# Four additions a weight pair move from VectorE to GpSimd, and the weight preparation around them shifts by one to two products

## The chip, the cores and the metric

The kernel runs on one core of a Trainium2 chip. Its time is device microseconds (us) of one execution, as the median over several runs. The engines are called by the letters of the profile: PE is TensorE (matrix products; PEld its weight loads), DVE is VectorE, ACT is ScalarE, POOL is GpSimd and SP is SyncE, which issues the transfers (DMAs).

## The reference

Retention attention over 8 sequences of 8 heads, followed by two feed-forward layers over its 4608 tokens, all in float32:

```
x = attention(q, k, v)                      # [4608, 512]
h = x @ w_in                                # [4608, 2048]
x2 = (h * cos(h)) @ w_out                   # [4608, 512]
z = max(max(x2 @ w1, x2 @ w2), x2 @ w3)     # [4608, 768]
out = z @ w_out2                            # [4608, 512]
```

## The kernel before, in words

**Tiles.** Tokens go in 9 blocks of 512. Every large product works on 2x2 quarters of its operands with seven products in place of eight (the names A11, A12, A22, S1 to S4 are quarters and their sums and differences). Each operand is split into a high and a low float32r part, and three matmuls (high by high, low by high, high by low) make one term.

**Stages**, in us of the profiled span: lead-in to about 95; attention and the first half of h to 346; the second half of h to 596; **x2** from 596 to 1001; the three branches (w1, w2, w3) to about 1405; the last product to the end. The change acts in x2, and a little in the branches.

**x2** (`phase_out`, kind "wo") goes through 36 groups: 9 blocks by 4 groups (k = 0 to 3) of the 2048 features. A group is seven products of 12 matmuls, in the order A11, A12, S4, S2, A22, S3, S1. The names of a group's tiles end in its k: `k_g_2` holds the quarters of group 2 as loaded. `build_out` prepares a group while the group before it is multiplied:

- two loads of `k_g` (SP, L364); two differences `ta_g` on POOL (L350); the high part `x_g` of A11 (ACT L741) and its low part (DVE L745);
- high parts `h_g` (ACT L749) and low parts `l_g` (DVE L754), for A12 and S4 straight from `k_g`, for S2 and A22 from `tb_g`, for S3 and S1 from `ta_g`;
- `tb_g`, two differences on DVE (L350), the first of which reads the first half of `ta_g`.

`finish_out` combines finished products on DVE (L794) and ACT (L801).

**Background conversions.** While the large products run, `background` turns weight pairs of the later stages into the seven operands of such a product. There are 24 conversions. Twelve belong to earlier stages and end before the step that changes (`if (kind, i) in plain: return`). Of the other twelve, nine run in x2, one a block (tiles `raw_b`, `fa_b`, `p_b`), and three in the branches (`raw_o`, `fa_o`, `p_o`). One conversion:

- load the first half of the raw weights (L165); widen on ACT (L171, L172), join on DVE (L176, L177), total on POOL (L183); then the same with the second half, whose load waits until the first total has read the tile;
- `add_up`: four additions and subtractions of quarters, 128x256 each (`sums`, L190 to L193);
- four pieces k = 0 to 3: high part on ACT (L200, L204, L207), low part on POOL (L216; L212 on DVE for k = 1), and a store to DRAM (L261).

**What sets the order.** `at(n, fn)` puts a step into a table and `tick()` closes a product: steps `at(n)` are issued n products from now, and within one product in the order in which they were entered. Each engine then works strictly in the order of issue, so a step that waits holds up all that stands behind it on its engine.

Of the kernel before, what the change touches and what calls it, by code (L numbers as in the profile page):

```python
# [101 lines left out]
def retention_ffn(ctx: ExitStack, tc: tile.TileContext, att, w_in, w_out, w123, w_out2, cst, out):  # L102
    nc = tc.nc
# [8 lines left out]
    def w14(name, dt=F32R):  # L112
        shape = [128, 7, 2, HB] if dt == F32R else [128, 7 * NB]
        return wpool.tile(shape, dt, tag="w", name=name)

    def x4(name, shape, dt=F32):
        return xpool.tile([128, *shape], dt, tag="x", name=name)
# [4 lines left out]
    def f32(t):  # L122
        return t.bitcast(F32)
# [13 lines left out]
    def at(n, fn):  # L137
        agenda.setdefault(slot[0] + n, []).append(fn)
# [25 lines left out]
    def load_raw(raw, kind, i, n):  # L164
        nc.sync.dma_start(out=raw, in_=source(kind, PAIRS[kind][i][n]).bitcast(U32))  # L165

    def widen(raw, t):

        r = raw.rearrange("p (n t) -> p n t", t=2)
        low, high = r[:, :, 0], r[:, :, 1]  # L170
        nc.scalar.activation(t.bitcast(F32), high.bitcast(F32), AF.Copy, scale=2.0**-111)  # L171
        nc.scalar.activation(low, low, AF.Copy, scale=2.0**-29)  # L172

    def join(raw, t):
        high = raw.rearrange("p (n t) -> p n t", t=2)[:, :, 1]
        nc.vector.tensor_scalar(out=t, in0=t, scalar1=3, scalar2=None, op0=ALU.logical_shift_left)  # L176
        nc.vector.scalar_tensor_tensor(  # L177
            out=high, in0=high, scalar=0x80000000, in1=t, op0=ALU.bitwise_and, op1=ALU.bitwise_or
        )

    def total(raw, dst, eng):
        r = raw.rearrange("p (n t) -> p n t", t=2)
        eng.tensor_tensor(out=dst.bitcast(U32), in0=r[:, :, 0], in1=r[:, :, 1], op=ALU.add)  # L183

    def quarters(kind, fa):
        return [fa[:, q] for q in PLACES[kind]]

    def sums(kind, fa, s, eng):
        a11, a12, a21, a22 = quarters(kind, fa)
        eng.tensor_tensor(out=s[:, 0], in0=a21, in1=a22, op=ALU.add)  # L190
        eng.tensor_tensor(out=s[:, 1], in0=s[:, 0], in1=a11, op=ALU.subtract)
        eng.tensor_tensor(out=s[:, 2], in0=a11, in1=a21, op=ALU.subtract)
        eng.tensor_tensor(out=s[:, 3], in0=a12, in1=s[:, 1], op=ALU.subtract)  # L193

    def piece_high(kind, fa, s, k, dst):

        if k == 0:
            step = PLACES[kind][1]
            src = fa[:, 0 : 2 * step : step] if step > 1 else fa[:, 0:2]
            nc.scalar.copy(dst[:, :, 0], src)  # L200
            return src
        if k == 1:
            src = quarters(kind, fa)[3]
            nc.scalar.activation(dst[:, 0, 0], src, AF.Copy, scale=-1.0)  # L204
            return src
        src = s[:, 2 * k - 4 : 2 * k - 2]
        nc.scalar.copy(dst[:, :, 0], src)  # L207
        return src

    def piece_low(k, src, dst, eng):  # L210
        if k == 1:
            nc.vector.scalar_tensor_tensor(  # L212
                out=dst[:, 0, 1], in0=src, scalar=-1.0, in1=f32(dst[:, 0, 0]), op0=ALU.mult, op1=ALU.subtract
            )
        else:
            eng.tensor_tensor(out=dst[:, :, 1], in0=src, in1=f32(dst[:, :, 0]), op=ALU.subtract)  # L216
# [5 lines left out]
    def background(kind, i, arena):  # L222

        st = {}

        def begin():
            if arena:
                w = w14(f"ar_{kind}{i}", F32)
                st["raw"] = w[:, : 2 * NB].bitcast(U32)
                st["fa"] = w[:, 2 * NB : 4 * NB].rearrange("p (q n) -> p q n", q=4)  # L230
                st["t"] = w[:, 6 * NB :].bitcast(U32)
            else:
                st["raw"] = x4(f"raw_{kind}{i}", [2 * NB], U32)
                st["fa"] = x4(f"fa_{kind}{i}", [4, HB])
                st["t"] = spare
            load_raw(st["raw"], kind, i, 0)

        def convert(n):
            return [
                lambda: widen(st["raw"], st["t"]),  # L240
                lambda: join(st["raw"], st["t"]),
                lambda: total(
                    st["raw"], st["fa"][:, 2 * n : 2 * n + 2].rearrange("p q n -> p (q n)"), nc.gpsimd
                ),
            ]

        def add_up():
            st["s"] = f32(st["raw"]).rearrange("p (q n) -> p q n", q=4)
            sums(kind, st["fa"], st["s"], nc.vector)

        def high(k):
            lo, hi = PIECE[k]
            st["p", k] = x4(f"p_{kind}{i}_{k}", [hi - lo, 2, HB], F32R)
            st["src", k] = piece_high(kind, st["fa"], st["s"], k, st["p", k])

        def low(k):
            piece_low(k, st["src", k], st["p", k], nc.gpsimd)

        def keep(k):
            lo, hi = PIECE[k]  # L260
            nc.sync.dma_start(out=stash[kind, i][:, lo:hi], in_=f32(st["p", k]))  # L261

        c0, c1 = convert(0), convert(1)
        at(0, begin)
        for n, fn in enumerate(c0):
            at(3 + n, fn)
        at(6, lambda: load_raw(st["raw"], kind, i, 1))
        for n, fn in enumerate(c1):
            at(9 + n, fn)
        if (kind, i) in plain:  # L270
            at(13, lambda: nc.sync.dma_start(out=plain[kind, i], in_=st["fa"]))
            return
        at(14, add_up)
        for k in range(4):
            at(15 + k, lambda k=k: high(k))
            at(16 + k, lambda k=k: low(k))
            at(18 + k, lambda k=k: keep(k))

    def split_pair(kind, i, fa, s):
        w = w14(f"w_{kind}{i}")  # L280
# [44 lines left out]
    def raw_operand(o, product):  # L325
        return {
            P_A11: lambda: o["k1"][:, 0],
            P_A12: lambda: o["k2"][:, 0],
            P_S4: lambda: o["k2"][:, 1],
            P_S1: lambda: o["ta"][:, 0],  # L330
            P_S3: lambda: o["ta"][:, 1],
            P_S2: lambda: o["tb"][:, 0],
            P_A22: lambda: o["tb"][:, 1],
        }[product]()
# [17 lines left out]
    def high(o, product):  # L352
        x = o[product] = x4(f"x_{o['name']}_{product}", [2, o["n"]], F32R)
        nc.scalar.copy(x[:, 0], raw_operand(o, product))

    def low(o, product, eng):
        x = o[product]
        eng.tensor_tensor(out=x[:, 1], in0=raw_operand(o, product), in1=f32(x[:, 0]), op=ALU.subtract)  # L358
# [335 lines left out]
    for j in range(1, NBLK):  # L694
        k = 4 * (j - 1)
        build_in(block_of(j), start_of(k + 1) + 7, start_of(k + 3) + 7, xsd[j], nc.gpsimd)
    back = [(k, i) for k, n in (("wi", 4), ("wo", 0), ("b", 0), ("o", 0)) for i in range(n, len(PAIRS[k]))]
    per = 14
    for j in range(NBLK - 2):
        at(per * j, lambda: background(*back.pop(0), True))  # L700
# [16 lines left out]
    for j in range(NBLK - 1):  # L717
        at(endA + per * j + 3, lambda j=j: load_operands(j + 1))
        if j < 5:
            at(endA + per * j + 1, lambda: background(*back.pop(0), True))  # L720
# [140 lines left out]
            ),  # L861
        )
    for i in range(len(back) - 3):
        at(28 * i + 5, lambda: background(*back.pop(0), False))
    for k in range(4):
        for p in range(2):
            at(28 * (NBLK - 1) + 7 * k + 8 + p, lambda k=k, p=p: take("b", 2 * k + p))
# [113 lines left out]
```

## Time and profile before

| | |
|---|---|
| median of 3 runs | 1564.41 us (1562.49 to 1566.82) |
| the profiled execution | 1566.85 us, span 1565.0 us |
| PE busy in the span | 1468.8 us (94%) |
| DVE busy | 1233.1 us (79%) |
| ACT busy | 728.8 us (47%) |
| POOL busy | 493.4 us (32%) |

Shares of the whole span mix stages with different limits; the stage x2, from 596 to 1001, is the one to read. In the rows below a timeline's row gives start and duration, both in us, then engine, line, operation and tiles, and in brackets the idle time of the engine ahead of it and what ended that. Rows of waits give the idle time in total, how often, and the longest. The names of operands carry no group number there; where a row belongs to a certain group, the text says so.

### The profile page before, as it was taken

How to read it: one execution, taken by the hardware profiler on the slowest of the kernel's cores; microseconds unless marked ns; L12 is line 12 of the kernel's file. 1: busy time of each engine (PE TensorE's matmuls, PEld its weight loads, DVE VectorE, ACT ScalarE, POOL GpSimd, SP SyncE). 2: the span in 40 equal slices, each digit the busy share in tenths (PEclk: the TensorE clock that was granted, in tenths of full speed). 3: DMA queues.
4: the chain of work that ended last, by engine and by line, in shares of the span. 5: the costliest groups of instructions: out<-in, count | busy, mean ns of one | idle time of the engine just before them, and what ended most of it. 6: DMA issues, size and time to landing. Idle time of an engine off the chain costs nothing. (4 is left out here: it accounts for less than half of the span.)

```text
span 1565.0 us, 30902 instructions
## 1 busy us (share of the span) xinstructions
PE 1468.8 (94%) x12506; PEld 1424.4 (91%) x12506; DVE 1233.1 (79%) x1611; ACT 728.8 (47%) x1214; POOL 493.4 (32%) x364
## 2 busy tenths in 40 slices
PE   7799999997998996899999999999999999998998
PEld 5698989996988996899999999899999999998998
DVE  6988989898878869899999999746554554538997
ACT  4465655565666665344443444434433333323332
POOL 3544444434333334455444445201110000003221
PEclk9999999997999997999999999999999999999999
DMA  7588888875998873545556656944332211153543
GB/s 287 202 307 316 313 295 301 304 256 212 330 339 303 326 276 132 183 165 177 191 188 209 206 168 253 390 176 142 129 100 83 68 46 50 68 193 137 176 164 133
DMA packets 83086, 324.47 MB, mean 207 GB/s; under 512 B 9216, under 2 KB 9216, under 8 KB 76928
## 3 DMA queue, kind: packets, MB, share of 16 engines
q1 hardware_dynamic: 82944, 322.51, 58.0%
q8 instruction: 98, 1.61, 0.4%
q14 instruction: 44, 0.36, 0.1%
HBM read 190.35 MB, written 132.12 MB: 206 GB/s over the span
## 5 line engine op out<-in xcount | busy, mean ns | idle before, releaser
L781 PE MATMUL wo<-h_g,w_wo 128*128 128x256 f32 x1728 | 317.9, 285 | 0.0
L781 PEld LDWEIGHTS wo<-h_g,w_wo 128*128 128x128 f32 x1728 | 273.0, 194 | 0.0
L781 PE MATMUL wo<-l_g,w_wo 128*128 128x256 f32 x864 | 250.3, 290 | 20.7 <-DVE l_g L754 20.1
L379 PE MATMUL d_b<-x_z,w_b 128*128 128x256 f32 x1944 | 250.1, 284 | 7.0 <-DVE s_b L403 4.9
L379 PEld LDWEIGHTS d_b<-x_z,w_b 128*128 128x128 f32 x1944 | 241.2, 193 | 7.9 <-DVE s_b L403 5.1
L781 PEld LDWEIGHTS wo<-l_g,w_wo 128*128 128x128 f32 x864 | 167.6, 194 | 27.3 <-DVE l_g L754 27.0
L446 POOL TENSOR_SCALAR t_a<-t_a 128x1024 f32<-128x1024 f32 x72 | 91.9, 1281 | 179.9 <-DVE t_a L445 138.2
L379 PE MATMUL d_a<-x_x,w_wi 128*128 128x256 f32 x864 | 126.1, 298 | 9.3 <-DVE x_x L358 7.4
L379 PE MATMUL b_b<-x_z,w_b 128*128 128x256 f32 x972 | 131.9, 284 | 2.0 <-DVE x_z L358 2.0
L379 PE MATMUL d_a<-x_y,w_wi 128*128 128x256 f32 x864 | 116.0, 292 | 18.5 <-DVE s_a L403 7.9
L379 PEld LDWEIGHTS d_a<-x_y,w_wi 128*128 128x128 f32 x864 | 110.5, 199 | 21.6 <-DVE s_a L403 8.1
L379 PEld LDWEIGHTS d_a<-x_x,w_wi 128*128 128x128 f32 x864 | 113.0, 199 | 14.2 <-DVE x_x L358 8.5
L379 PEld LDWEIGHTS b_b<-x_z,w_b 128*128 128x128 f32 x972 | 123.5, 192 | 2.2 <-DVE x_z L358 2.2
L350 POOL TENSOR_TENSOR ta_m<-k_m 128x512 f32<-128x512 f32 (+1 forms) x18 | 18.9, 1048 | 334.0 <-DMA k_m<-mq 273.6
L749 ACT CAST h_g<-tb_g 128x1024 fp32r<-128x1024 f32 x36 | 37.8, 1049 | 179.6 <-DVE tb_g L350 174.1
L781 PE MATMUL o<-h_m,w_o 128*128 128x256 f32 x648 | 117.4, 283 | 0.0
L453 DVE TENSOR_TENSOR s_a<-s_a,t_a 128x1024 f32<-128x1024 f32 x72 | 98.7, 1385 | 15.4 <-ACT t_a L450 15.1
L403 DVE TENSOR_TENSOR s_b<-s_b,b_b 128x512 f32<-128x512 f32 (+1 forms) x45 | 28.5, 634 | 93.7 <-PE b_b L379 92.1
L781 PEld LDWEIGHTS o<-h_m,w_o 128*128 128x128 f32 x648 | 101.1, 192 | 0.0
L445 DVE SCALAR_TENSOR_TENSOR t_a<-s_a,t_a 128x1024 f32<-128x1024 f32 x72 | 97.6, 1375 | 0.4 <-ACT t_a L441 0.4
L450 ACT ACTIVATE t_a<-t_a 128x1024 f32<-128x1024 f32 x72 | 75.7, 1060 | 46.5 <-POOL t_a L446 46.5
L350 POOL TENSOR_TENSOR ta_g<-k_g 128x512 f32<-128x512 f32 x36 | 51.5, 1431 | 128.5 <-DMA k_g<-gq 128.5
(168 smaller groups left out, 3200.0 us busy)
## 6 DMA issues: line engine op xcount, KB each, us to landing
u<-att SPq DMA_DIRECT2D x36, 1024.0 KB, 8.1
gq<-s_a SPq DMA_DIRECT2D x72, 512.0 KB, 6.7
k_g<-gq SPq DMA_DIRECT2D x72, 512.0 KB, 6.6
xs<-x_x SPq DMA_DIRECT2D x63, 512.0 KB, 8.0
x_y<-xs SPq DMA_DIRECT2D x63, 512.0 KB, 7.7
w_b<-st_b SPq DMA_DIRECT2D x8, 1792.0 KB, 14.0
st_b<-p_b SPq DMA_DIRECT2D x27, 512.0 KB, 2.9
raw_b<-w SPq DMA_DIRECT2D x18, 512.0 KB, 5.6
```

What stands on the lines that cost most here:

```text
L350: eng.tensor_tensor(out=d, in0=a, in1=b, op=ALU.subtract)
L379: nc.tensor.matmul(h[:, p * HB : (p + 1) * HB], a, b, start=first and p == 0 and i == 0, stop=i == len(terms) - 1, skip_group_check=True,)
L403: nc.vector.tensor_tensor(out=dst, in0=dst, in1=b[:, :n], op=ALU.add)
L445: nc.vector.scalar_tensor_tensor(out=r, in0=s, scalar=INV2PI, in1=st["t"], op0=ALU.mult, op1=ALU.subtract)
L446: nc.gpsimd.tensor_scalar(out=r, in0=r, scalar1=R_MOST, scalar2=R_LEAST, op0=ALU.min, op1=ALU.max)
L450: nc.scalar.activation(r, r, AF.Sin, scale=TURN, bias=HALF_PI)
L453: nc.vector.tensor_tensor(out=s, in0=s, in1=f32(st["t"]), op=ALU.mult)
L749: nc.scalar.copy(h, o[pairs[k][2]])
L781: nc.tensor.matmul(b[:, mt * HB : (mt + 1) * HB], a, v, start=first and mt == 0 and p == 0 and i == 0, stop=last and p == len(ws) - 1 and ...
```

## The change

The four sums of `add_up` are issued on POOL in place of DVE (12 conversions, 48 instructions). The four pieces come later: the high part of piece k at 16, 17, 19, 20 products from the conversion's start in place of 15 to 18, and low part and store likewise. The nine conversions of x2 start two products earlier within their block; those in the branches start where they did.

```
         def add_up():
             st["s"] = f32(st["raw"]).rearrange("p (q n) -> p q n", q=4)
-            sums(kind, st["fa"], st["s"], nc.vector)
+            sums(kind, st["fa"], st["s"], nc.gpsimd)
...
         at(14, add_up)
         for k in range(4):
-            at(15 + k, lambda k=k: high(k))
-            at(16 + k, lambda k=k: low(k))
-            at(18 + k, lambda k=k: keep(k))
+            at(16 + k + k // 2, lambda k=k: high(k))
+            at(17 + k + k // 2, lambda k=k: low(k))
+            at(19 + k + k // 2, lambda k=k: keep(k))
...
     for i in range(len(back) - 3):
-        at(28 * i + 5, lambda: background(*back.pop(0), False))
+        at(28 * i + 3, lambda: background(*back.pop(0), False))
```

POOL, from the differences of group 1 to the first low part, in one block of x2 before (a row is line, operation, tiles, shape):

```order
266 L350 TENSOR_TENSOR ta_g_1_9166<-k_g_1_9102 128x512
267 L350 TENSOR_TENSOR ta_g_1_9166<-k_g_1_9104,k_g_1_9102 128x512
268 L350 TENSOR_TENSOR ta_g_2_9285<-k_g_2_9224 128x512
269 L350 TENSOR_TENSOR ta_g_2_9285<-k_g_2_9226,k_g_2_9224 128x512
270 L183 TENSOR_TENSOR fa_b_9244<-raw_b_9243 128x512
271 L350 TENSOR_TENSOR ta_g_3_9404<-k_g_3_9344 128x512
272 L350 TENSOR_TENSOR ta_g_3_9404<-k_g_3_9346,k_g_3_9344 128x512
273 L183 TENSOR_TENSOR fa_b_9244<-raw_b_9243 128x512
274 L216 TENSOR_TENSOR p_b_0_9492<-fa_b_9244,p_b_0_9492 128x2x256
```

The same stretch of POOL after the change:

```order
288 L183 TENSOR_TENSOR fa_b_9208<-raw_b_9207 128x512
289 L350 TENSOR_TENSOR ta_g_2_9290<-k_g_2_9227 128x512
290 L350 TENSOR_TENSOR ta_g_2_9290<-k_g_2_9229,k_g_2_9227 128x512
291 L183 TENSOR_TENSOR fa_b_9208<-raw_b_9207 128x512
292 L350 TENSOR_TENSOR ta_g_3_9405<-k_g_3_9344 128x512
293 L350 TENSOR_TENSOR ta_g_3_9405<-k_g_3_9346,k_g_3_9344 128x512
294 L190 TENSOR_TENSOR raw_b_9207<-fa_b_9208 128x256
295 L191 TENSOR_TENSOR raw_b_9207<-raw_b_9207,fa_b_9208 128x256
296 L192 TENSOR_TENSOR raw_b_9207<-fa_b_9208 128x256
297 L193 TENSOR_TENSOR raw_b_9207<-fa_b_9208,raw_b_9207 128x256
298 L216 TENSOR_TENSOR p_b_0_9478<-fa_b_9208,p_b_0_9478 128x2x256
```

Each of the two totals (L183) stood behind the differences `ta_g` of a group and now stands ahead of them; the four sums now follow the differences of group 3.

DVE before, from the last low part of group 2 to the low parts of group 3:

```order
888 L754 TENSOR_TENSOR l_g_2_9374<-ta_g_2_9285,h_g_2_9341 128x1024
889 L176 TENSOR_SCALAR spare<-spare 128x512
890 L177 SCALAR_TENSOR_TENSOR raw_b_9243<-raw_b_9243,spare 128x512
891 L745 TENSOR_TENSOR x_g_3_9407<-k_g_3_9344,x_g_3_9407 128x512
892 L350 TENSOR_TENSOR tb_g_3_9437<-k_g_3_9346,ta_g_3_9404 128x512
893 L754 TENSOR_TENSOR l_g_3_9439<-k_g_3_9346,h_g_3_9423 128x1024
894 L350 TENSOR_TENSOR tb_g_3_9437<-tb_g_3_9437,k_g_3_9346 128x512
895 L190 TENSOR_TENSOR raw_b_9243<-fa_b_9244 128x256
896 L191 TENSOR_TENSOR raw_b_9243<-raw_b_9243,fa_b_9244 128x256
897 L192 TENSOR_TENSOR raw_b_9243<-fa_b_9244 128x256
898 L193 TENSOR_TENSOR raw_b_9243<-fa_b_9244,raw_b_9243 128x256
899 L754 TENSOR_TENSOR l_g_3_9478<-tb_g_3_9437,h_g_3_9454 128x1024
```

The same stretch of DVE after:

```order
868 L176 TENSOR_SCALAR spare<-spare 128x512
869 L177 SCALAR_TENSOR_TENSOR raw_b_9207<-raw_b_9207,spare 128x512
870 L754 TENSOR_TENSOR l_g_2_9378<-ta_g_2_9290,h_g_2_9342 128x1024
871 L745 TENSOR_TENSOR x_g_3_9408<-k_g_3_9344,x_g_3_9408 128x512
872 L350 TENSOR_TENSOR tb_g_3_9441<-k_g_3_9346,ta_g_3_9405 128x512
873 L754 TENSOR_TENSOR l_g_3_9443<-k_g_3_9346,h_g_3_9423 128x1024
874 L350 TENSOR_TENSOR tb_g_3_9441<-tb_g_3_9441,k_g_3_9346 128x512
875 L754 TENSOR_TENSOR l_g_3_9480<-tb_g_3_9441,h_g_3_9458 128x1024
```

The second join (L176, L177) now comes ahead of the last low part of group 2, and the four sums are gone. The first join has likewise moved ahead of the `x_g` of group 2 (it stood behind it), and on ACT the first widening (L171, L172) stands ahead of the high parts `x_g` and `h_g` of group 2, directly behind the two `h_g` of group 1. On SP the first raw load goes out ahead of the `k_g_2` loads in place of behind them.

## Rows read from the trace of the kernel before

**Rows 1.** The page: busy time by engine, and a costly group of instructions.

```profile
PE 1468.8 (94%) x12506; PEld 1424.4 (91%) x12506; DVE 1233.1 (79%) x1611; ACT 728.8 (47%) x1214; POOL 493.4 (32%) x364
...
L781 PE MATMUL wo<-l_g,w_wo 128*128 128x256 f32 x864 | 250.3, 290 | 20.7 <-DVE l_g L754 20.1
```

**Rows 2.** Busy time by stretch: PE, PEld, DVE, ACT, POOL; clock, DMA share, GB/s.

```profile
872.79:915.99 43.20, 42.07 (x336) 41.86 (x336) 39.93 (x41) 19.02 (x25) 20.70 (x13) 0.96 0.56 190
...
898.33:915.99 17.66, 16.53 (x138) 16.32 (x137) 17.59 (x18) 6.87 (x10) 12.09 (x8) 1.00 0.35 126
```

**Rows 3.** Waits of DVE from 872.79 to 915.99.

```profile
DVE l_g L754 <- ACT h_g L749: 2.3, 2, 1.2
```

**Rows 4.** Timeline of PE: A12 and S4 of group 3, A12 of the next block.

```profile
904.38 0.40 PE L781 MATMUL wo<-h_g,w_wo 128*128 128x256 f32 x2
...
905.82 0.40 PE L781 MATMUL wo<-h_g,w_wo 128*128 128x256 f32 x2
...
915.99 0.39 PE L781 MATMUL wo<-l_g,w_wo 128*128 128x256 f32 x1 [1.14 <-DVE l_g L754]
```

**Rows 5.** Timeline of DVE, from 884 to 909.

```profile
884.02 1.93 DVE L754 TENSOR_TENSOR l_g<-tb_g,h_g 128x1024 fp32r<-128x1024 f32 x1 [1.17 <-ACT h_g L749]
885.87 2.32 DVE L754 TENSOR_TENSOR l_g<-ta_g,h_g 128x1024 fp32r<-128x1024 f32 x1
...
890.38 2.07 DVE L754 TENSOR_TENSOR l_g<-k_g,h_g 128x1024 fp32r<-128x1024 f32 x1
...
896.50 0.42 DVE L176 TENSOR_SCALAR spare<-spare 128x512 uint32<-128x512 uint32 x1
897.00 0.69 DVE L177 SCALAR_TENSOR_TENSOR raw_b<-raw_b,spare 128x512 uint32<-128x512 uint32 x1
...
901.19 2.06 DVE L754 TENSOR_TENSOR l_g<-k_g,h_g 128x1024 fp32r<-128x1024 f32 x1
903.17 0.68 DVE L350 TENSOR_TENSOR tb_g<-tb_g,k_g 128x512 f32<-128x512 f32 x1
903.77 0.41 DVE L190 TENSOR_TENSOR raw_b<-fa_b 128x256 f32<-128x256 f32 x1
...
905.23 1.22 DVE L754 TENSOR_TENSOR l_g<-tb_g,h_g 128x1024 fp32r<-128x1024 f32 x1
...
907.50 0.69 DVE L794 SCALAR_TENSOR_TENSOR o_wo<-wo,u_wo 128x512 f32<-128x512 f32 x1
```

**Rows 6.** Timeline of POOL, from 883 to 909.

```profile
883.57 1.30 POOL L350 TENSOR_TENSOR ta_g<-k_g 128x512 f32<-128x512 f32 x1 [3.61 <-DMA k_g<-gq]
...
889.99 1.36 POOL L183 TENSOR_TENSOR fa_b<-raw_b 128x512 uint32<-128x512 uint32 x1 [2.89 <-DVE raw_b L177]
...
898.98 1.74 POOL L350 TENSOR_TENSOR ta_g<-k_g,k_g 128x512 f32<-128x512 f32 x1
900.68 1.49 POOL L183 TENSOR_TENSOR fa_b<-raw_b 128x512 uint32<-128x512 uint32 x1
906.60 2.15 POOL L216 TENSOR_TENSOR p_b<-fa_b,p_b 128x512 fp32r<-128x512 f32 x1 [4.44 <-ACT p_b L200]
```

**Rows 7.** Timeline of ACT, from 883 to 905.

```profile
883.89 1.05 ACT L749 CAST h_g<-ta_g 128x1024 fp32r<-128x1024 f32 x1
...
887.03 0.68 ACT L172 ACTIVATE raw_b<-raw_b 128x512 uint32<-128x512 uint32 x1
...
903.94 1.05 ACT L749 CAST h_g<-tb_g 128x1024 fp32r<-128x1024 f32 x1 [4.02 <-DVE tb_g L350]
```

**Rows 8.** POOL groups by shape: busy us, mean ns; idle before.

```profile
L350 POOL TENSOR_TENSOR ta_m<-k_m,k_m 128x256 f32<-128x256 f32 x9 | 7.7, 851 | 1.2 <-DMA k_m<-mq 1.1
L350 POOL TENSOR_TENSOR ta_m<-k_m 128x256 f32<-128x256 f32 x9 | 7.1, 790 | 53.5 <-DMA k_m<-mq 33.6 <-PE o L781 13.0 <-DVE o_o L794 6.9
L183 POOL TENSOR_TENSOR fa_o<-raw_o 128x512 uint32<-128x512 uint32 x6 | 6.2, 1039 | 126.1 <-DVE raw_o L177 126.1
```

**Rows 9.** Waits from 1001 to 1380, the branches.

```profile
ACT x_z L354 <- DMA st_o<-p_o: 5.9, 3, 2.4
```

## Prediction

> **What bounds the kernel now.** The page comes first: TensorE is busy 94% of the span, so only what makes it wait, or ends waits, can count. Its costliest wait in x2 is for `l_g` from VectorE [rows 1]. The busy time by stretch says why: in one block, 872.79 to 915.99, VectorE works 39.93 us of 43.20 [rows 2]. A product that does not wait takes 1.44 us (A12 of group 3 begins at 904.38, the next at 905.82 [rows 4]), so the 28 products of a block need 40.3 us, and the block takes 43.2. VectorE's waits are the next view: 2.3 us of its idle time in that block are two waits for ScalarE's `h_g` [rows 3]; nothing it waits for comes from TensorE. And in the last 17.66 us of the block, the part that the change rebuilds, VectorE is busy 17.59 [rows 2]. The timeline of TensorE shows the end of this chain: the second product of the next block stands still until 915.99, when `l_g` is there [rows 4]. So VectorE sets the pace of x2, and whatever makes it later between 884 and 916 lengthens the block. Waits of the other engines need no more reading.
>
> One more reading decides the prices. VectorE and GpSimd stretch each other: `l_g` takes 1.22 alone (905.23) and 2.07, 2.06, 2.32 where GpSimd works at the same time [rows 5]; GpSimd's difference takes 1.30 at 883.57 and 1.74 at 898.98, its total 1.04 with VectorE elsewhere and 1.36 to 1.49 here [rows 6, 8]. The surplus is about the other engine's instruction. I read it as taking turns for instructions of VectorE with two tiles to read. L794, which reads one tile and a product's accumulator, keeps 0.69 at 907.50 within GpSimd's 2.15 us low part [rows 5, 6]. If the engines did not exclude each other, four sums of 0.65 to 0.85 (below) would take no turns from it, and of the 3.3 us a conversion that the walk below gives, 2.6 to 3.4 would be gone: the second rival. The Trainium skill, "SBUF — State Buffer", section "Who interferes with whom", has it that such an instruction of VectorE and one of GpSimd that reads shut each other out, the first to issue holding the other up for its whole length. By that rule the turns below stand, and the surplus in these rows agrees.
>
> **The change part by part.** Prices are net of the 0.08 us by which rows of one engine overlap (903.17 + 0.68 against 903.77): `l_g` 1.15, a 128x512 on VectorE 0.6, the join 0.5 + 0.6 [rows 5]; `ta_g` 1.3, the total 1.04 [rows 6, 8]; a widening of two 1.25, `h_g` 1.0 [rows 7]. The trace has no such sum on GpSimd. From below it is half of the 1.30 of a 128x512, 0.65; the nearest rows are differences of exactly 128x256, 0.79 and 0.85 on average, with collisions in them [rows 8]. I take 0.65 to 0.85.
>
> *The first total ahead of the differences of group 2.* Before, `ta_g_2` runs at 883.57, as soon as its quarters land, and the total waits for the join until 889.99 [rows 6]. Now GpSimd reaches `ta_g_2` only behind the total, and the total needs the join. The join is issued behind both `l_g` of group 1. These gain: without `ta_g_2` beside them, 884.02 + 2 × 1.15 = 886.3. Join to 887.4 (its widening follows ScalarE's `h_g` that ends at 884.94, done at 886.2 [rows 7], in time if the earlier raw load has landed, as it should). `x_g` to 888.0, total to 889.05, first difference to 890.35. Then `tb_g` 0.6, second difference 1.3 and `l_g` 1.15 take turns in some order: 893.4. Before, this `l_g` ended at 890.38 + 2.07 = 892.45. So **+0.95 us**; the cover is what group 1's `l_g` gained, without it it would be +2.9.
>
> *The second total ahead of the differences of group 3.* Second `tb_g` to 894.0, ScalarE's `h_g` to 895.1, `l_g` to 896.25, ScalarE's other `h_g` and the widening to 897.3, the join to 897.9 (before 897.69 [rows 5], but then with the last `l_g` of group 2 already done). From there `l_g` 1.15, `x_g` 0.6, total 1.04 and first difference 1.3 exclude each other: 902.0. `tb_g`, second difference and `l_g` as above: 905.05. GpSimd's first sum is ready by then and gets its turn ahead of `l_g` or not: 905.05 to 905.9, where `l_g` ended at 901.19 + 2.06 = 903.25. So **+1.8 to +2.65**, and TensorE, which began this A12 at 904.38 [rows 4], waits about a microsecond here.
>
> *The sums.* VectorE loses four instructions, 903.77 to 905.23, 1.46 us [rows 5]. But they lay in a gap: ScalarE's `h_g` from `tb_g` ran 903.94 to 904.99 [rows 7], and the next `l_g` began at 905.23. Taken out, they bring 0.2 us. On GpSimd they meet the second `tb_g` and the two `l_g` of group 3. From 905.7: `tb_g` 0.6, three further sums of 0.65 to 0.85, two `l_g` 2.3 in turns, 910.55 to 911.15; with the sums wholly inside ScalarE's wait, 909.65. Before, 907.50 + 0.08. So **+2.1 to +3.6**, I take +3.3, since GpSimd has the sums ready when `l_g` comes.
>
> *The pieces.* In x2 their first two come one product earlier, the others where they were. The low parts stay on GpSimd and still lie beside `l_g` and L212; drawn out from 1.30 alone they are already (2.15 [rows 6]). With less time between sums and pieces I add **0 to 0.6, take 0.3**. The stores are not waited for in x2.
>
> *The next block.* From 907.5 VectorE goes on without a pause to the `l_g` that TensorE awaits at 915.99 [rows 2, 4], so no slack eats the delay: about **+3.6 us a conversion, 32.4 for nine**.
>
> *The branches.* VectorE isn't the bound there, so four sums less bring nothing; the pieces come one to two products later. ScalarE waits three times, 5.9 us, for a stored piece to come back [rows 9]; most is covered by products already prepared. From below that stays so; from above that wait grows by half and TensorE sees all of it, 3 us. I take the middle, **+1.5**.
>
> Sum: 1566.85 + 32.4 + 1.5 = 1600.8 for the profiled execution, which lies 2.4 above the median; so **1598 us**. The bounds: nine times 2.1 alone, +19, to nine times 4.2 and 3, +41: 1583 to 1605.
>
> The Trainium skill, "GPSIMD Engine Reference", section "Engine selection", advises VectorE for elementwise work and calls GpSimd about twice as slow with two inputs. Here 1.30 against 0.68 for 128x512 agrees [rows 5, 6]. By that factor a sum is 0.82, an estimate, near the upper of my two, and the time some 3 us more.
>
> **The rivals.**
>
> *Only the sums collide, the totals do no harm.* If VectorE and GpSimd fill each other's gaps better than my turns, so that `ta_g_2` and `ta_g_3` are ready when `tb_g` comes, what is left is four sums of 0.65 to 0.85 in VectorE's way less the 1.46 us: 1.1 to 1.9 a conversion, +10 to +17: 1574 to 1582, **1578**. For it: the first half costs under 1 us even by my walk. Against: the second total needs a join that ends at 897.9, and `ta_g_3` was early before.
>
> *Nothing measurable.* The change then does nothing for VectorE but empty a gap that ScalarE's `h_g` sets anyway, and the collisions lie in gaps too: **1564**, within 5 us. For it: the 0.2 us above. Against: 17.59 of 17.66 us leave no gaps.
>
> *Faster.* VectorE is the bound and gives up four instructions of some 0.41 us a conversion [rows 5]; if GpSimd does the sums wholly in VectorE's remaining waits, nine blocks gain 1.64 each, 15 us: **1549**. It comes if the differences end before VectorE comes to `tb_g`: in group 2 before some 888, in group 3 before 899. `ta_g_2` alone ended 5 us ahead of its reader before, which speaks for it; that it must now follow a join that VectorE itself issues just ahead of that reader speaks against it.
>
> **How the numbers follow.** The serial chain through GpSimd 0.62, only collisions 0.15, nothing 0.08, faster 0.15. About 0.3% (4.7 us) is what can be told from no change here. Hence slower 0.77, same 0.08, faster 0.15. The likeliest's own range is 1583 to 1605. The range for 8 in 10 takes in the cases of collisions and no change below it, and 3 us above for sums at the full price: 1560 to 1608; what it leaves out is the faster case and a little above.
>
> **What would show it.** In the profile after: x2 near 437 us in place of 405 (it ran from 596 to 1001); GpSimd's `ta_g_2` released by VectorE's join and its total, no longer by the load; VectorE idle 2 to 3 us ahead of each first `tb_g` of groups 2 and 3, waiting for `ta_g`; `l_g` of group 1 back at 1.2 us; sums at 0.65 to 0.85 on GpSimd; TensorE's wait for `l_g` at A12 of group 3 as well as of group 0, some 50 us in all in place of 20.7. It would be wrong if VectorE shows no wait for `ta_g`, or if its delay of group 3 is gone by the next block's A12.

## The result and the profile after

The changed kernel takes 1586.72 us (median of 4 runs, 1585.33 to 1588.36), the kernel before 1565.52 us on the same chips; the ratio is 1.0128, 95% interval 1.0111 to 1.0145. It is slower, by 21 us where 34 were forecast, inside the range given.

Its profiled execution has a span of 1585.9 us. From TensorE's timeline, x2 (start of its first product to the start of the first of the branches) takes 416.8 us in place of 404.4, and the branches (from there to the first of the last product) 427.2 in place of 421.3. What comes before x2, which the change does not touch, differs by 1.6 us between the two executions, and in all executions below it lies between 591.4 and 597.7; so stages are compared here, not times from the start.

The page's busy times and its group of waiting matmuls, as in [rows 1]:

```profile
PE 1474.3 (93%) x12506; PEld 1429.1 (90%) x12506; DVE 1209.2 (76%) x1563; ACT 726.5 (46%) x1214; POOL 541.2 (34%) x412
...
L781 PE MATMUL wo<-l_g,w_wo 128*128 128x256 f32 x864 | 251.3, 291 | 28.3 <-DVE l_g L754 27.9
```

VectorE has 24 us less to do in all, GpSimd 48 us more, and TensorE waits 8 us more for `l_g` (27.9 us against 20.1).

The busy time by stretch, for the block that answers to 872.79 to 915.99 in [rows 2]:

```profile
881.95:927.03 45.08, 41.47 (x336) 40.61 (x336) 37.70 (x37) 18.91 (x25) 24.83 (x17) 1.00 0.53 181
```

The waits of VectorE in that block, as in [rows 3]:

```profile
DVE l_g L754 <- ACT h_g L749: 3.5, 3, 1.2
DVE tb_g L350 <- POOL ta_g L350: 3.4, 2, 2.2
DVE spare L176 <- ACT spare L171: 0.3, 1, 0.3
```

VectorE works 2.2 us less in a block that is 1.9 us longer, and now waits: 3.4 us for `ta_g`, and one wait more for ScalarE's `h_g`, in the place where the sums had been. The granted clock was 1.00 in this block and 0.96 in that of [rows 2], so the clock is not what makes it longer. TensorE's timeline gives the length of a block best; the wait for `l_g` at A12 of group 0, in the second block and in the ninth:

```profile
656.76 0.38 PE L781 MATMUL wo<-l_g,w_wo 128*128 128x256 f32 x1 [2.01 <-DVE l_g L754]
...
972.10 0.39 PE L781 MATMUL wo<-l_g,w_wo 128*128 128x256 f32 x1 [1.99 <-DVE l_g L754]
```

Seven blocks in 315.34 us are 45.05 a block. The same two waits before:

```profile
655.20 0.38 PE L781 MATMUL wo<-l_g,w_wo 128*128 128x256 f32 x1 [1.99 <-DVE l_g L754]
...
959.62 0.38 PE L781 MATMUL wo<-l_g,w_wo 128*128 128x256 f32 x1 [1.99 <-DVE l_g L754]
```

That is 43.49 a block. So a conversion costs **1.56 us** here, not 3.6; the first block, counted from its own A12 (597.89 before, 599.47 after), takes 57.3 us in both and shows no cost.

VectorE's timeline over the same work as [rows 5] (893.22 here answers to 884.02 there, 9.20 earlier):

```profile
893.22 1.23 DVE L754 TENSOR_TENSOR l_g<-tb_g,h_g 128x1024 fp32r<-128x1024 f32 x1 [1.17 <-ACT h_g L749]
894.36 1.22 DVE L754 TENSOR_TENSOR l_g<-ta_g,h_g 128x1024 fp32r<-128x1024 f32 x1
...
899.43 1.76 DVE L350 TENSOR_TENSOR tb_g<-k_g,ta_g 128x512 f32<-128x512 f32 x1 [2.18 <-POOL ta_g L350]
901.12 1.21 DVE L754 TENSOR_TENSOR l_g<-k_g,h_g 128x1024 fp32r<-128x1024 f32 x1
...
906.08 0.69 DVE L177 SCALAR_TENSOR_TENSOR raw_b<-raw_b,spare 128x512 uint32<-128x512 uint32 x1
...
910.54 1.77 DVE L350 TENSOR_TENSOR tb_g<-k_g,ta_g 128x512 f32<-128x512 f32 x1 [1.18 <-POOL ta_g L350]
912.23 1.75 DVE L754 TENSOR_TENSOR l_g<-k_g,h_g 128x1024 fp32r<-128x1024 f32 x1
913.91 1.22 DVE L350 TENSOR_TENSOR tb_g<-tb_g,k_g 128x512 f32<-128x512 f32 x1
916.30 1.22 DVE L754 TENSOR_TENSOR l_g<-tb_g,h_g 128x1024 fp32r<-128x1024 f32 x1 [1.17 <-ACT h_g L749]
917.44 1.22 DVE L754 TENSOR_TENSOR l_g<-ta_g,h_g 128x1024 fp32r<-128x1024 f32 x1
918.58 1.52 DVE L212 SCALAR_TENSOR_TENSOR p_b<-fa_b,p_b 128x256 fp32r<-128x256 f32 x1
...
924.70 2.28 DVE L754 TENSOR_TENSOR l_g<-k_g,h_g 128x1024 fp32r<-128x1024 f32 x1
```

GpSimd's timeline of the same stretch, as in [rows 6]:

```profile
896.88 1.27 POOL L183 TENSOR_TENSOR fa_b<-raw_b 128x512 uint32<-128x512 uint32 x1 [7.72 <-DVE raw_b L177]
898.11 1.29 POOL L350 TENSOR_TENSOR ta_g<-k_g 128x512 f32<-128x512 f32 x1
...
906.91 1.90 POOL L183 TENSOR_TENSOR fa_b<-raw_b 128x512 uint32<-128x512 uint32 x1 [6.26 <-DVE raw_b L177]
908.77 1.74 POOL L350 TENSOR_TENSOR ta_g<-k_g 128x512 f32<-128x512 f32 x1
...
911.72 1.19 POOL L190 TENSOR_TENSOR raw_b<-fa_b 128x256 f32<-128x256 f32 x1
912.98 1.59 POOL L191 TENSOR_TENSOR raw_b<-raw_b,fa_b 128x256 f32<-128x256 f32 x1
914.54 1.19 POOL L192 TENSOR_TENSOR raw_b<-fa_b 128x256 f32<-128x256 f32 x1
915.69 0.74 POOL L193 TENSOR_TENSOR raw_b<-fa_b,raw_b 128x256 f32<-128x256 f32 x1
```

The serial chain is there as forecast: join, total, difference, `tb_g`, and VectorE waits at 899.43 and 910.54. But look at what became of the instructions around these waits. `l_g` of group 1 took 1.93 and 2.32 and takes 1.23 and 1.22; that of group 2 took 2.07 and takes 1.21 [rows 5]. And the sums, 911.72 to 916.43, meet one `l_g` (1.75) and the second `tb_g` (1.22) and are all but over when VectorE's wait for ScalarE ends at 916.30.

In the branches, ScalarE's timeline shows what was not there before:

```profile
1089.58 0.62 ACT L207 CAST p_o<-raw_o 128x512 fp32r<-128x512 f32 x1
1092.69 0.62 ACT L207 CAST p_o<-raw_o 128x512 fp32r<-128x512 f32 x1 [2.49 <-DVE s_b L886]
1095.55 0.37 ACT L411 COPY s_b<-d_b 128x256 f32<-128x256 f32 x1 [2.23 <-POOL p_o L216]
```

and TensorE's timeline what comes of it, three times in all:

```profile
1095.97 1.42 PE L379 MATMUL d_b<-x_z,w_b 128*128 128x256 f32 x6 [1.87 <-ACT s_b L411]
```

The high part of the last piece waits for VectorE's L886, the low part on GpSimd follows it, a copy of the branch's own sums (L411) waits for that, and TensorE for the copy: 2.15 us from one matmul's start to the next.

### The profile page after: what moved, and what is told of

It reads as the page before. It is cut to its first block, busy times and chain, and to the rows that moved or that the text cites. A ratio compares the mean times of both kernels' runs of the same rounds, so it can differ in the third digit from the quotient of the medians.

```text
span 1585.9 us, 30901 instructions
## 1 busy us (share of the span) xinstructions
PE 1474.3 (93%) x12506; PEld 1429.1 (90%) x12506; DVE 1209.2 (76%) x1563; ACT 726.5 (46%) x1214; POOL 541.2 (34%) x412
## 5 line engine op out<-in xcount | busy, mean ns | idle before, releaser
L781 PE MATMUL wo<-l_g,w_wo 128*128 128x256 f32 x864 | 251.3, 291 | 28.3 <-DVE l_g L754 27.9
L379 PE MATMUL d_b<-x_z,w_b 128*128 128x256 f32 x1944 | 251.7, 285 | 12.4 <-ACT s_b L411 5.6
L403 DVE TENSOR_TENSOR s_b<-s_b,a_b 128x512 f32<-128x512 f32 (+1 forms) x45 | 28.6, 635 | 88.3 <-PE a_b L379 79.1
```

Of the source, the lines that this page charges most:

```text
L379: nc.tensor.matmul(h[:, p * HB : (p + 1) * HB], a, b, start=first and p == 0 and i == 0, stop=i == len(terms) - 1, skip_group_check=True,)
L403: nc.vector.tensor_tensor(out=dst, in0=dst, in1=b[:, :n], op=ALU.add)
L781: nc.tensor.matmul(b[:, mt * HB : (mt + 1) * HB], a, v, start=first and mt == 0 and p == 0 and i == 0, stop=last and p == len(ws) - 1 and ...
```

## The experiments

Each stage is read from TensorE's timeline, as above; the ratio is to the kernel before on the same chip.

| kernel | time, us | ratio (95% interval) | x2, us | branches, us |
|---|---|---|---|---|
| before | 1565.52 | | 404.4 | 421.3 |
| changed | 1586.72 | 1.0128 (1.0111 to 1.0145) | 416.8 | 427.2 |
| e1 sums alone | 1575.65 | 1.0047 (1.0032 to 1.0061) | 412.1 | 420.5 |
| e2 start alone | 1579.46 | 1.0076 (1.0053 to 1.0098) | 420.1 | 418.1 |
| e3 pieces alone | 1575.03 | 1.0050 (1.0031 to 1.0069) | 406.1 | 425.8 |
| e4 chain cut | 1584.82 | 1.0115 (1.0094 to 1.0135) | 414.7 | 427.0 |
| e5 sums twice | 1602.06 | 1.0224 (1.0194 to 1.0253) | 435.5 | 424.5 |
| e6 second difference on VectorE | 1545.42 | 0.9861 (0.9838 to 0.9884) | 383.8 | 422.5 |
| e7 e6 and e1 | 1552.12 | 0.9907 (0.9884 to 0.9930) | 391.4 | 422.4 |
| e8 e6 and the change | 1563.04 | 0.9970 (0.9956 to 0.9983) | 392.9 | 427.3 |
| e9 branch pieces back | 1580.08 | 1.0086 (1.0063 to 1.0109) | 418.8 | 421.6 |
| e10 both differences on VectorE | 1551.34 | 0.9904 (0.9888 to 0.9920) | 388.1 | 423.6 |

In x2, e9 is the code of the changed kernel, and is 1.9 us longer in its execution; so differences of some 2 us in a stage tell nothing by themselves. Theory A in the expectations is the forecast's likeliest case, D its first rival; the letters that come later are said there.

**e1, the sums alone.** The sums on GpSimd, and nothing else of the change.

```
-            sums(kind, st["fa"], st["s"], nc.vector)
+            sums(kind, st["fa"], st["s"], nc.gpsimd)
```

> The four sums go to GpSimd, and nothing else changes: the conversions begin where they did before, the pieces come when they did, the totals stay behind the differences. In the changed kernel x2 (first to last product) took 12.5 us more than before and what follows x2 some 7 us more. Theory A, the totals ahead of the differences make x2 slow: x2 longer by 0 to 4 us, no wait of VectorE for ta_g. Rival D, the sums in VectorE's way make it slow: x2 longer by 10 to 17 us. For what follows x2: if the sums on GpSimd are late there, 6 us more; if it is the later pieces, nothing. In all A with pieces: 1565 to 1570 us; D: 1575 to 1583.

x2 is 7.7 us longer: more than A allowed, less than D asked. The branches have none of the later stops. TensorE's timeline, the same two waits as above:

```profile
655.02 0.39 PE L781 MATMUL wo<-l_g,w_wo 128*128 128x256 f32 x1 [2.51 <-DVE l_g L754]
...
966.80 0.38 PE L781 MATMUL wo<-l_g,w_wo 128*128 128x256 f32 x1 [2.29 <-DVE l_g L754]
```

44.54 us a block, 1.05 more than before. The sums do lie in VectorE's way: beside them the second `tb_g` of group 3 takes 1.22 us in place of 0.68, and the `l_g` behind ScalarE's last high part 1.76 in place of 1.22. VectorE is busy 371.4 us of x2 against 373.7 before, although 36 sums of 0.42 us, 15 us in all, have left it: the other instructions have grown by some 12.7 us, 1.4 a conversion.

**e2, the earlier start alone.**

```
-        at(28 * i + 5, lambda: background(*back.pop(0), False))
+        at(28 * i + 3, lambda: background(*back.pop(0), False))
```

> Only the start of the nine conversions in x2 comes two products earlier; the sums stay on VectorE and the pieces where they were from the start of a conversion. The totals now stand ahead of the differences on GpSimd. Theory A: VectorE waits some 3.4 us a block for ta_g as in the changed kernel, x2 longer by 8 to 13 us, about 1575 us. Rival D: no sums in the way, x2 within 3 us of before, about 1565 us. What follows x2 is as before under both.

x2 is 15.7 us longer, beyond both; from 656.55 to 970.86, the same place in the second block and the ninth, a block takes 44.90, 1.41 more than before, and most of the rest comes behind that, in the last block (46.3 from there to the branches, 40.9 before). It speaks against D as D was put. VectorE waits 22.2 us for `ta_g`, but the run does not isolate A: with this start the sums, still on VectorE, stand ahead of the first `tb_g` of group 3, beside GpSimd's differences. VectorE's timeline:

```profile
907.77 1.51 DVE L190 TENSOR_TENSOR raw_b<-fa_b 128x256 f32<-128x256 f32 x1
909.32 1.40 DVE L191 TENSOR_TENSOR raw_b<-raw_b,fa_b 128x256 f32<-128x256 f32 x1
910.64 1.52 DVE L192 TENSOR_TENSOR raw_b<-fa_b 128x256 f32<-128x256 f32 x1
912.08 0.41 DVE L193 TENSOR_TENSOR raw_b<-fa_b,raw_b 128x256 f32<-128x256 f32 x1
```

and GpSimd's:

```profile
907.26 1.75 POOL L350 TENSOR_TENSOR ta_g<-k_g 128x512 f32<-128x512 f32 x1
908.96 1.48 POOL L350 TENSOR_TENSOR ta_g<-k_g,k_g 128x512 f32<-128x512 f32 x1
910.40 1.47 POOL L216 TENSOR_TENSOR p_b<-fa_b,p_b 128x512 fp32r<-128x512 f32 x1
```

A sum that takes 0.41 us takes 1.5 beside an instruction of GpSimd, and each waits for one of these three to end (908.96 + 1.48 = 910.44, where L191 gets its turn; L190 has its at 909.01, L192 at 911.87). The two engines alternate, one instruction each. The Trainium skill, "SBUF — State Buffer", section "Who interferes with whom", has it that a VectorE instruction with two SBUF inputs and a GpSimd instruction that reads block each other for a whole instruction; these rows agree, 1.40 to 1.52 us in place of 0.41.

**e3, the later pieces alone** (low part and store likewise; the ninth conversion of x2 starts two products earlier).

```
-            at(15 + k, lambda k=k: high(k))
+            at(16 + k + k // 2, lambda k=k: high(k))
...
-        at(28 * i + 5, lambda: background(*back.pop(0), False))
+        at(28 * i + (5 if i < 8 else 3), lambda: background(*back.pop(0), False))
```

> Only the four pieces come one to two products later; the sums stay on VectorE and the conversions begin as before (the ninth in x2 two products earlier, or its last store would come too late). Theory P, the later pieces stop TensorE in the branches: three stops of about 2.1 us, what follows x2 longer by 6 us. Rival S, the sums on GpSimd do that: no stops, 0 us. x2 by theory A and by D within 3 us of before. In all P: 1571 us, S: 1565 us.

x2 is within its scatter of before. The three stops of 2.15 us are there with the sums on VectorE; the branches are 4.5 us longer. P holds for the branches; the time is 4 us above its 1571.

**e4, the chain cut.** The changed kernel, each total entered behind the differences of its group.

```
-            at(3 + n, fn)
+            at(3 + n + (n == 2 and not arena), fn)
...
-            at(9 + n, fn)
+            at(9 + n + 2 * (n == 2 and not arena), fn)
```

> The changed kernel with the two totals of a conversion entered one and two products later, so that on GpSimd each stands behind the differences of its group again; the sums stay on GpSimd behind the differences of group 3, all else is as in the changed kernel. Theory A: VectorE's wait for ta_g is gone and x2 is back within 4 us of before; with the 7 us behind x2 about 1573 to 1577 us. Rival D: the sums collide as before, x2 stays 10 to 13 us longer, about 1586 us.

The waits of VectorE in all of x2, 28.1 us of which were for `ta_g` in the changed kernel:

```profile
DVE l_g L754 <- ACT h_g L749: 30.4, 26, 1.2
DVE spare L176 <- ACT spare L171: 5.1, 9, 2.7
DVE raw_b L177 <- DVE spare L176: 0.5, 1, 0.5
```

The wait that A called the cause is gone, all of it, and x2 is 2.1 us shorter, hardly more than its scatter. TensorE's two waits for `l_g`:

```profile
656.07 0.58 PE L781 MATMUL wo<-l_g,w_wo 128*128 128x256 f32 x1 [1.99 <-DVE l_g L754]
...
968.24 0.38 PE L781 MATMUL wo<-l_g,w_wo 128*128 128x256 f32 x1 [2.53 <-DVE l_g L754]
```

44.60 us a block, about as in e1. A falls as the main cause: cutting the chain gives back 0.45 us a block, and x2 stays 10.3 us longer than before, as D had it (10 to 13). VectorE has the same 1563 instructions in both kernels, and is busy 1234.8 us in all here, 1209.2 in the changed kernel: what it had waited it now spends in longer instructions. So a third theory, E: the two engines take turns, and what GpSimd does beside VectorE costs VectorE its time on GpSimd, in whichever order it comes, as a wait or as a longer instruction.

**e5, the sums twice.** e1 with the four sums of x2 done a second time.

```
             sums(kind, st["fa"], st["s"], nc.gpsimd)
+            if kind == "b":
+                sums(kind, st["fa"], st["s"], nc.gpsimd)
```

> As the run with only the sums on GpSimd, and in x2 each of its nine conversions does the four sums twice, with the same result. In that run x2 took 412.1 us from its first product to the first of the branches (before 404.4). Theory E, GpSimd and VectorE take turns, so that work on GpSimd costs VectorE its time on GpSimd: four more of 0.74 us, 3.0 a conversion, less at most the 1 us of ScalarE's high part in which VectorE waits anyway: 18 to 27 us more, x2 430 to 439, about 1594 to 1603 us in all. Rival H, sums on GpSimd are hidden and only their order counts: under 8 us more, x2 under 420.

x2 is 23.4 us longer than in e1, within E's range. TensorE's two waits:

```profile
657.79 0.39 PE L783 MATMUL wo<-l_g,w_wo 128*128 128x256 f32 x1 [4.08 <-DVE l_g L756]
...
989.40 0.39 PE L783 MATMUL wo<-l_g,w_wo 128*128 128x256 f32 x1 [4.08 <-DVE l_g L756]
```

(The lines of this kernel are numbered two higher.) 47.37 us a block, 2.83 more than e1: 0.71 for each of four further sums. Alone, in the branches, a sum lasts 0.73 to 0.74 on GpSimd (their median there in the changed kernel for three of the four). So H falls. But the number alone does not show that the engines take turns: VectorE is busy 1235.0 us in all, only 6.1 more than in e1 (1228.9). Most of the price comes as waits, and by another way. ScalarE's timeline, then VectorE's, behind the second round of sums of one block:

```profile
933.62 0.62 ACT L207 CAST p_b<-raw_b 128x512 fp32r<-128x512 f32 x1 [2.23 <-POOL raw_b L191]
934.79 0.75 DVE L747 TENSOR_TENSOR x_g<-k_g,x_g 128x512 fp32r<-128x512 f32 x1 [1.81 <-ACT x_g L743]
937.99 1.73 DVE L352 TENSOR_TENSOR tb_g<-k_g,ta_g 128x512 f32<-128x512 f32 x1 [1.12 <-POOL ta_g L352]
```

ScalarE's high part of a piece waits for the sums, the `x_g` that stands behind it on ScalarE comes late, and VectorE waits for that; then it waits for the `ta_g` that stands behind the sums on GpSimd. In x2 VectorE's waits for ScalarE's `x_g` are 17.2 us (5.0 in e1) and those for `ta_g` 10.1 (1.2). So e5 shows that further sums on GpSimd are not hidden; it does not tell E's turns from a chain of waits. The evidence for the turns is in the longer instructions of e1 and e2, and of e6 below.

**e6, the second `ta_g` difference on VectorE**, in the kernel before: if E holds, GpSimd's share should shrink.

```
-        at(offs[0], lambda: difference(o, 3, nc.gpsimd))
+        if name[0] != "g":
+            at(offs[0], lambda: difference(o, 3, nc.gpsimd))
...
         at(offs[2], lambda: difference(o, 4, nc.vector))
+        if name[0] == "g":
+            at(offs[2], lambda: difference(o, 3, nc.vector))
```

> The kernel before, in x2 with the second of a group's two ta_g differences on VectorE in place of GpSimd, behind the second tb_g, where VectorE waits for ScalarE's high part in three groups of four; the sums stay on VectorE behind it. Theory E: GpSimd no longer takes 1.30 us of turns a group, and VectorE does it in 0.6 us of a wait: 0.7 to 1.3 a group, 2.8 to 5.2 a block, of which TensorE's own 40.3 us a block leaves 2.9: x2 shorter by 12 to 26 us, 1540 to 1555 us in all. Rival V, VectorE is the bound by the length of its own list: 0.6 us a group more, less what fits the waits, x2 longer by 0 to 21 us, 1566 to 1588 us.

x2 is 20.6 us shorter, and the kernel is faster than the one before and the changed one. VectorE has 36 instructions more, 24.5 us at 0.68, and is busy 1218.2 us in all in place of 1233.1: its other instructions take 39.4 us less, 1.1 for each difference that has left GpSimd, where one takes 1.3 alone. That is busy time and not waits (for `ta_g` VectorE waited 1.2 us in all of x2 before), so here it is the turns that show. Its timeline where the difference stands now:

```profile
901.42 0.68 DVE L350 TENSOR_TENSOR tb_g<-tb_g,k_g 128x512 f32<-128x512 f32 x1
902.02 0.68 DVE L350 TENSOR_TENSOR ta_g<-k_g,k_g 128x512 f32<-128x512 f32 x1
903.28 1.23 DVE L754 TENSOR_TENSOR l_g<-tb_g,h_g 128x1024 fp32r<-128x1024 f32 x1 [0.57 <-ACT h_g L749]
```

It fills 0.6 of the 1.17 us that VectorE waited here for ScalarE. The page's group of waiting matmuls, 20.7 us of waits before and 8.1 here:

```profile
L784 PE MATMUL wo<-l_g,w_wo 128*128 128x256 f32 x864 | 246.7, 286 | 8.1 <-DVE l_g L754 8.1
```

**e7, e6 and the sums on GpSimd**; **e8, e6 in the changed kernel**; both with the edits shown.

> The second ta_g difference on VectorE as in the run named second_vector, and the sums on GpSimd with nothing else of the change. Theory E: the sums' turns now meet less of GpSimd's other work; x2 within 8 us of second_vector, longer by 0 to 8; 1540 to 1560 us in all. Rival V: about 1566 to 1590 us.

> The changed kernel with the second ta_g difference on VectorE. Theory E: what delays tb_g there is GpSimd's serial work, 1.3 us shorter a group now: x2 shorter than in the changed kernel by 15 us or more, 1565 to 1572 us in all with the 6 us of the branches still in it. Rival V: the changed kernel's 1587 us or more.

In e7 x2 is 7.6 us longer than in e6, as e1's was against before (7.7). In e8 it is 24.0 us shorter than in the changed kernel; the time is 2 us under E's range, and slightly better than before. VectorE still waits 27.1 us for `ta_g` there (28.1 in the changed kernel), so x2 did not get shorter by the way that the expectation named, a shorter wait. With and without the moved difference the sums on GpSimd lose; V falls.

**e9, the pieces of the branches back.** The changed kernel, with the old places for the kind "o".

```
+            d = 1 + k // 2 if kind == "b" else 0
-            at(16 + k + k // 2, lambda k=k: high(k))
+            at(15 + k + d, lambda k=k: high(k))
```

(and likewise low part and store)

> The changed kernel, with the four pieces at their old places in the three conversions of the branches alone; their sums stay on GpSimd, and x2 is as in the changed kernel. Theory P, the later pieces stop TensorE three times for 2.15 us there: the stops are gone, the branches 421 us in place of 427.2, 1580 to 1582 us in all. Rival S, the sums on GpSimd have a part in it: stops stay, 1584 us or more.

The stops are gone, the branches are at 421.6, the time 6.6 us lower. The delay of the pieces is the cause of the branches' part; the timeline above puts it on the last of them.

**e10, both differences on VectorE.**

```
-        at(offs[0], lambda: difference(o, 1, nc.gpsimd))
-        at(offs[0], lambda: difference(o, 3, nc.gpsimd))
+        if name[0] != "g":
+            at(offs[0], lambda: difference(o, 1, nc.gpsimd))
+            at(offs[0], lambda: difference(o, 3, nc.gpsimd))
...
+        if name[0] == "g":
+            at(offs[2], lambda: difference(o, 1, nc.vector))
         at(offs[2], lambda: difference(o, 2, nc.vector))
...
+        if name[0] == "g":
+            at(offs[2], lambda: difference(o, 3, nc.vector))
```

> The kernel before, in x2 with both ta_g differences of a group on VectorE, the first just ahead of the first tb_g, the second behind the second tb_g. With the second alone there a block took 41.2 us, against 40.3 for TensorE's 28 products. Theory E: the first takes 1.30 us of turns on GpSimd and 0.6 on VectorE, where nothing hides it; up to 0.7 a group less, of which 0.9 a block are left to gain: x2 shorter by 0 to 8 us than with the second alone, 1537 to 1546 us in all. Rival V: 0.6 a group more on VectorE's list, up to 2.4 a block, 1546 to 1566 us.

x2 is 4.3 us longer than in e6. Here V's range holds the time, and E's is missed: E is too strong if it counts every microsecond on GpSimd. The first difference on GpSimd lies partly beside VectorE's waits and L794, which keeps its 0.69 us beside GpSimd [rows 5, 6]; on VectorE nothing covers it. So what decides should be how much of either engine's instruction lies beside a wait of the other; that is argued from these rows, and no run varies it alone.

## Why the prediction was right in its direction, and 11 us too high

*That it gets slower, and where:* right. VectorE is the bound, the four instructions that leave it filled a wait for ScalarE (a third such wait stands in their place), and GpSimd's total now stands in front of `tb_g`.

*The first total, +0.95 at `l_g` of group 2:* this `l_g` ends at 902.33 - 9.20 = 893.13, forecast 893.4. Right.

*The second total, +1.8 to +2.65 at `l_g` of group 3:* the join ends at 906.77 - 9.20 = 897.57 (897.9), this `l_g` at 913.98 - 9.20 = 904.78 (905.05 to 905.9). So +1.5, a little under the range. TensorE's wait for A12 there came as forecast, 1.21 us in this block, though not in every one.

*The sums, taken as +3.3:* here the forecast failed. The last `l_g` of group 3 ends at 918.66 - 9.20 = 909.46, where 909.65 had been given for sums wholly inside ScalarE's wait. So +1.9. The step was: "I take +3.3, since GpSimd has the sums ready when `l_g` comes". Ready they were, but early enough that the last ended at 915.69 + 0.74 = 916.43, when the `l_g` that had waited for ScalarE began (916.30): they met the `l_g` and `tb_g` ahead of that wait, and ran on within it.

*The pieces, +0.3, and the next block:* L212 did grow from 0.93 to 1.52, but the `x_g` behind it shrank from 1.78 to 1.19 us. The pieces cost nothing. TensorE's wait for the next block's `l_g` ends at 927.03 - 9.20 = 917.83 in place of 915.99 [rows 4]: +1.84 in this block, +1.56 over seven. "No slack eats the delay" held from the end of the sums on.

*The shares:* the walk put 1.8 to 2.65 on the chain and the rest on the sums, and in this trace the chain's part is indeed the larger. But the two do not add up as in the walk. The sums alone cost 1.05 us a block (e1), near the first rival's 1.1 to 1.9; the earlier start alone 1.41, with the sums on VectorE (e2); both together 1.56; and cutting the chain in the changed kernel gives back only 0.45 (e4). Before, VectorE paid for GpSimd's work in `l_g` of 2 us and more; in the changed kernel it pays in waits; with the chain cut it pays in longer instructions again.

*The branches, +1.5 (0 to 3):* measured +5.9 in the profile, 6.6 between the changed kernel and e9. The step looked at the wait for stored pieces (L354 on the store) and had no term for what the last piece holds up on its way. Why ScalarE's copies wait for L886 and for L216 is argued only: they share no data, so it should be the slots of their tiles; no run here took more slots.

*The sum:* x2 +12.4 where +32.4 stood, the branches +5.9 where +1.5 stood. So x2 lies under the likeliest case's own lower bound of +19, inside the first rival's +10 to +17, and the branches above their upper bound of 3. That the time is inside the likeliest case's 1583 to 1605 all the same is luck, two misses of opposite sign: with the branches at +1.5 it would have been some 1582. Of the 20 us too much in x2, 16 are nine times the difference between 3.6 and the 1.84 of the block shown; the rest is that 1.84 is more than the mean, and that the first block costs nothing.

*The signs:* the `l_g` of group 1 back at 1.2, `ta_g_2` behind the join and the total, and the wait at A12 of group 3 came. VectorE's idle time ahead of `tb_g` was 2.18 and 1.18 us in place of 2 to 3 each. The sums took 0.74 to 1.59 in x2 in place of 0.65 to 0.85, and TensorE's wait for `l_g` was 28.3 us in place of some 50.

## What to carry to other kernels

Where two engines take turns, as these two did here, do not expect a gain from moving an instruction off the busy one unless the other runs it beside a wait, or is quicker at it; count what it lasts on the new engine, 0.74 us against 0.41 here, and take off what the old place had hidden. A wait that shows in the profile need not be what it costs: cut it, and see whether the time comes back as longer instructions (25.6 of 28.1 us in e4). And when a background step comes later, follow who waits on that engine behind its last piece, not only who reads its result.

## What the runs showed of the hardware

VectorE's 128x256 sum took 0.41 us with GpSimd idle and 1.40 to 1.52 beside GpSimd's instructions (e2); on GpSimd the same sum took 0.74 alone and up to 1.76 beside VectorE's (e4). VectorE, busy 92% of x2 before, took 36 instructions more in e6 and the stage ended 20.6 us earlier: they no longer stretched its other instructions from GpSimd (39.4 us less), and they filled waits for ScalarE.
